# Pooled-key attention with a mixture of adapters: queries of chunks 4 to 7 turned by DMA, scores moved into the start, and the second batch's preparation re-timed

## The chip, the cores and the metric

The kernel runs on one core of a Trainium2 chip. The engines of the core run side by side, each through its own instruction list in order: TensorE (PE in the profile; its weight loads are PEld), VectorE (DVE), ScalarE (ACT), GpSimd (POOL), and SyncE (SP), which here issues nearly all DMAs. The metric is the device time of one execution in microseconds, taken as the median of several executions. The profile is one execution with every instruction recorded.

## The reference

There are four batches of 12288 queries with 128 columns. The keys and values of a batch are its kv image, averaged over 4x4 blocks to 768 rows and multiplied by `w_sr`. Softmax attention is followed by eight rank-16 adapters, of which each token uses its two best:

```python
kv_pool = kv.reshape(B, H // r, r, W // r, r, C).mean(axis=(2, 4))
kv_flat = kv_pool.reshape(B, -1, C) @ w_sr
a = softmax(scale * (q @ kv_flat.transpose(0, 2, 1)))
x = a @ kv_flat
logits = x @ w_gate             # the two largest of 8, softmax over them: w
out = x + sum over the two experts e of w[e] * (x @ A[e]) @ B[e]
```

## The kernel before

**Tiling.** The 49152 queries are cut into 96 chunks of 512, 24 per batch. A batch's keys are three tiles of 256 rows. One unit of score work, `scores(c, r)` (L295), multiplies chunk c's turned queries `qT` with key tile r on PE (two matmuls into a bank pair `sg`; there are two such pairs) and ACT takes the exponentials out of it into `tt` (L304). `weigh(c, h)` (L306) multiplies half of the exponentials with the values `vext` into `xps`, 12 matmuls each. `normalise(c)` (L319) is DVE work: a reciprocal (L322), the scaled copy `xn` (L326), and four searches for the largest logits, `top` (L333). Since `xps` exists once, the next chunk's first `weigh` waits for `xn`.

**The main loop** (L653) runs over c = 2 to 94; one pass is called period c here. It takes three units of score work from a list in order (`next_scores`), weighs chunk c-1, normalises it, turns the chunk before it for the adapters (`turned`, L373), and, with a lag of nine periods at first, multiplies by the adapters' first factor (`gated_hidden`) and second (`up`). The chunk's adapter weights go as follows. In every even period POOL runs `gate` for two chunks (five short instructions, L342 to L346), which needs DVE's `top` of that period. In the odd period after it, behind the second unit of score work, ACT runs a tanh over the result (`gate_tanhs`, L358). DVE then turns it (L402), and it goes out and comes back through DRAM.

**Queries.** A half of 1024 queries (two chunks) is loaded as fp32 by SP (`load_q`), cast to fp16 by POOL (`cast_q`, L107, in even periods behind `gate`), and turned by a DMA transpose on SP's queue (`turn_q`, L114). There are two fp32 buffers `q32`, so a load waits on SP's queue for the cast of two halves before. The first eight chunks do not go this way: they come in two loads `q0` and `q1`, and PE turns them (`queries`, L567), with ACT (chunks 0 to 3) or DVE (4 to 7) copying them to `qT`.

**Keys and values.** Each tile of a batch's kv image is loaded in four rows of 512 KB. Three additions join the rows (`sum_row`, L173) and two join the columns (`sum_cols`, L177, L178). DVE does this for batch 0, before the loop; POOL does it for the later ones. `plan(b)` (L255) fixes the periods: `at` for the loads, `sm` for the sums, `st` for the three steps on PE and ACT, which are the pooled transpose with its copy (`kp`, L189 and L191, at the period in `st`), values (L197, L199, two periods later) and keys (L205, L207, three periods later). In the loop `prep(c)` issues loads and sums, behind the gate and the cast of that period. `squares` (L236) is POOL work on values that a range check at the end needs.

**The start.** Tiles 0 to 2 of batch 0 become keys one after the other as their rows land (`tile_keys`, `tile_values`, written out from L603 on). Between them stand the query turns, the first scores and, as filler, plain matmuls (`warm`). Nine units of score work stand before the loop, and the loop takes one extra unit at the end of periods 6 and 8 (L717).

Of the kernel before, what the change touches and what calls it, by code (L numbers as in the profile page):

```python
# [10 lines left out]
FP32 = mybir.dt.float32  # L11
# [4 lines left out]
AF = mybir.ActivationFunctionType  # L16
# [5 lines left out]
def kernel(  # L22
# [10 lines left out]
    nc = tc.nc  # L33
    P = 128
    B, N, C = q.tensor.shape
# [5 lines left out]
    NTOK = 512  # L41
# [56 lines left out]


    def load_q(i):  # L100
        q32[i] = qpool.tile([P, 2, NS * C], FP32, tag="q32", name="q32", bufs=2)
        nc.sync.dma_start(q32[i], qflat[i * HROWS:(i + 1) * HROWS].rearrange(
            "(k p s) c -> p k (s c)", p=P, s=NS))

    def cast_q(i):
        q16[i] = qpool.tile([P, HROWS], F16, tag="q16", name="q16", bufs=3)
        nc.gpsimd.tensor_copy(q16[i], q32[i].rearrange("p k n -> p (k n)"))  # L107

    def new_qT(i):
        qT[i] = qpool.tile([P, 2 * NS, P], F16, tag="qT", name="qT", bufs=5)  # L110
# [1 line left out]
    def turn_q(i):  # L112
        new_qT(i)
        nc.sync.dma_start(qT[i], q16[i], transpose=True)  # L114
# [3 lines left out]
    for t in range(NT):  # L118
        load_kv(0, t)
        if t == 0:  # L120

            nc.sync.dma_start(q0, qflat[0:GROWS].rearrange("(k p s) c -> p k s c", p=P, s=NS))
    nc.sync.dma_start(q1, qflat[GROWS:2 * GROWS].rearrange("(k p s) c -> p k s c", p=P, s=NS))

    w_in = const.tile([P, P], FP32)
    nc.scalar.dma_start(w_in, w_sr)
# [53 lines left out]
    def stile(name):  # L180
        return ps_s.tile([P, 2, NTOK], FP32, tag="sg", name=name)
# [27 lines left out]
    def tile_keys(t, between=lambda: None):  # L209

        k = slice(2 * t * P, 2 * (t + 1) * P)
        kp_ps = ps_t.tile([P, 2 * P], FP32, tag="tp", name="kp_ps")
        for u in range(2):
            mm(kp_ps[:, u * P:(u + 1) * P], kvt[0, t][:, 0, u, 0:C], id_f32, is_transpose=True,
               start=(u == 0), stop=(u == 1), skip_group_check=True)
        if t < NT - 1:
            nc.scalar.activation(kpT[0][:, k], kp_ps, AF.Copy)
        else:
            nc.vector.tensor_copy(kpT[0][:, k], kp_ps)
        between()  # L220
        k_ps = mtile([P, 2 * P], name="k_ps")
        mm(k_ps, w_sr_sb, kpT[0][:, k], start=True, stop=True)
        nc.scalar.activation(kfT[0][:, k], k_ps, AF.Copy)

    def tile_values(t):
        v_ps = mtile([P, 2, C + E], name="v_ps")
# [28 lines left out]
    def plan(b):  # L255
        c0 = CPB * (b - 1)
        if b == 1:
            at = [2, 2, 3, 4, 5, 6, 6, 8, 9, 10, 10, 12]
            sm = [5, 5, 7, 9, 9, 11, 13, 13, 15]
            st = [10, 14, 18]  # L260
        else:
            at = [-11, -9, -7, -5, -5, -3, -1, 1, 1, 3, 5, 7]
            sm = [-3, -1, 1, 3, 5, 7, 9, 11, 13]
            st = [4, 10, 16]
        for i, k in enumerate(at):
            loads.setdefault(c0 + k, []).append((b, i // 4, i % 4))
# [28 lines left out]
    def scores(c, r):  # L295
        b = c // CPB
        if r == 0:
            tt[c] = ttpool.tile([P, NJ, NTOK], F16, tag="tt", name="tt")
        qc = qT[c // 2][:, c % 2 * NS:(c % 2 + 1) * NS].rearrange("p s t -> p (s t)")
        sg = stile("sg")  # L300
        for k in range(2):
            j = 2 * r + k
            mm(sg[:, k], kfT[b][:, j * P:(j + 1) * P], qc, start=True, stop=True)  # L303
        nc.scalar.activation(tt[c][:, 2 * r:2 * r + 2], sg, AF.Exp, bias=0.0, scale=scale)  # L304
# [253 lines left out]

    for i in range(4):
        new_qT(i)

    def queries(g, k, t):

        for i in range(NS):
            mm(t[:, i * P:(i + 1) * P], (q0, q1)[g][:, k, i], id_f32, is_transpose=True,  # L567
               start=(i == 0), stop=(i == NS - 1), skip_group_check=True)
        qt = qT[2 * g + k // 2][:, k % 2 * NS:(k % 2 + 1) * NS].rearrange("p s t -> p (s t)")
        if g == 0:  # L570
            nc.scalar.activation(qt, t, AF.Copy)
        else:
            nc.vector.tensor_copy(qt, t)
# [13 lines left out]
    a_bf = const.tile([P, P], BF16)  # L587
    b_half = const.tile([P, P], FP32)
    b_bf = const.tile([P, P], BF16)
    load_q(4)  # L590
    load_q(5)
    cast_q(4)
    for t in range(NT):
        for d in range(1, 4):
            sum_row(0, t, d, nc.vector)
        sum_cols(0, t, nc.vector)
        if t == 0:
            nc.vector.tensor_copy(a_bf.rearrange("p (r e) -> p e r", e=E),
                                  a_f.rearrange("p (e r) -> p e r", e=E))
# [3 lines left out]
    tile_keys(0, lambda: queries(0, 0, x_bank()))  # L603
    queries(0, 1, x_bank())
    scores(0, 0)
    tile_values(0)
    queries(0, 2, x_bank())
    scores(1, 0)
    queries(0, 3, x_bank())
    scores(2, 0)  # L610
    scores(3, 0)
    warm(8)
    tile_keys(1)
    warm(2)
    scores(0, 1)
    tile_values(1)
    scores(1, 1)
    weigh(0, 0)
    warm(2)
    tile_keys(2, lambda: queries(1, 0, stile("q_ps")[:, 0]))  # L620
    queries(1, 1, t_bank())
    scores(0, 2)
    tile_values(2)
    scores(2, 1)
    queries(1, 2, t_bank())
    weigh(0, 1)
    scores(1, 2)
    normalise(0)

    todo = [(x, r) for x in range(2, NCH) for r in range(3) if (x, r) not in ((2, 0), (2, 1), (3, 0))]

    def next_scores():
        if todo:
            scores(*todo.pop(0))

    NQ = NCH // GRP

# [12 lines left out]
    for c in range(2, NCH - 1):  # L653
        b, k = divmod(c, CPB)
        if c in fetched and lag(2 * fetched[c] + 1) > 8:
            load_gates(fetched[c])
        if c % 2 == 0 and c // 2 + 3 < 2 * NQ:
            turn_q(c // 2 + 3)
        if c % 2 and (c + 11) // 2 < 2 * NQ:
            load_q((c + 11) // 2)  # L660
        if c == 2:
            load_q(6)
        next_scores()
        if c == 2:
            queries(1, 3, t_bank())
        weigh(c - 1, 0)
        if c == NCH - 2:
            down(c - 4, stile("h_ps")[:, 0])
            apply_gate(c - 4)
        next_scores()  # L670
        if c >= 3 and c % 2 == 1:
            gate_tanhs((c - 3) // 2)
        for x in made.get(c, ())[:-1]:
            gated_hidden(x, t_bank())
        for x in ups.get(c, ()):
            up(x, None if x == ups[c][-1] else t_bank())
# [12 lines left out]
        _, evacuate = turned("x", c - 2)  # L689
        if c == NCH - 2:  # L690
            _, evacuate_h = turned("h", c - 4, stile("t_ps")[:, 0])
        next_scores()
        prep(c)
        if k in (17, 19, 21) and b + 1 < B:
            if b == 0:
                squares(0, (k - 17) // 2)
            squares(b + 1, (k - 17) // 2)
        if c in (32, 40, 56, 80):
            ranges((32, 40, 56, 80).index(c))
        a = slice(0, CUT * NS)  # L700
        if CUT < c <= CUT + 3:
            count_ok(a, c - CUT - 1, flags[:, 0:1])
        elif c == CUT + 4:
            values_ok()
        elif c == CUT + 5:
            count_sum(1)
        for x in made.get(c, ())[-1:]:
            gated_hidden(x)
        if c in sent:
            send_gates(sent[c])  # L710
        if c == NCH - 2:
            down(c - 3, stile("h_ps")[:, 0])
            apply_gate(c - 3)
        evacuate(c == NCH - 2)
        if c == NCH - 2:
            evacuate_h(True)
        if c in (6, 8):  # L717
            next_scores()

# [285 lines left out]
```

## Time and profile before

| | |
|---|---|
| median of 3 runs | 381.48 us (381.07 to 382.75) |
| the profiled execution | 382.61 us, its span 380.8 us |
| PE busy | 362.9 us (95%) |
| ACT, DVE, POOL busy | 311.1, 301.7, 224.4 us |
| DMA moved | 100.47 MB, mean 264 GB/s |

In rows of the timeline the first number is the start in us from the span's start and the second the length; in square brackets stands how long the engine had been idle before and what ended that. Rows of one kind that follow each other are merged, with their count at xN. PE's matmuls overlap in the pipeline, so a row is longer than the time by which it delays the next one. SPq is SP's queue issuing a DMA. In the view by windows each row has the stretch, its length, the busy time of each engine in it, the granted PE clock, the DMA share and GB/s.

### The profile page before, as it was taken

The numbers are of one execution on the slowest core, as the hardware profiler recorded it, in microseconds if no ns is written. First come the engines' busy times: TensorE is split into PE (matmuls) and PEld (weight loads), VectorE is DVE, ScalarE is ACT, GpSimd is POOL, SyncE is SP. The second block draws the span as 40 slices with busy tenths as digits, with TensorE's granted clock in tenths as the row PEclk, the third lists the DMA queues.
The fourth block names the chain that finished last, engine by engine and source line by source line (L and its number), as shares of the span: only waits on it lengthen the run. The fifth ranks groups of instructions, "written<-read, shape, count | busy, mean of one in ns | idle before, by whom it ended". The sixth has DMA issues, their size and how long they took to land.

```text
span 380.8 us, 10632 instructions
## 1 busy us (share of the span) xinstructions
PE 362.9 (95%) x3962; PEld 267.7 (70%) x3963; DVE 301.7 (79%) x951; ACT 311.1 (82%) x392; POOL 224.4 (59%) x374
## 2 busy tenths in 40 slices
PE   4989989999999999999999999999999999999993
PEld 1447757677777777777777777777777777767682
DVE  2686556878788888888888888888888898898983
ACT  1547999888888888888888988988888888888853
POOL 1002699996898877764689877755524335232244
PEclk9999999999999999999999999999999999999998
DMA  8996799999999999999999999999899799883325
GB/s 253 364 386 205 203 271 303 300 310 256 365 296 302 309 326 259 312 288 320 320 289 304 338 279 299 278 246 243 175 298 256 196 226 243 182 220 119 136 86 195
DMA packets 93465, 100.47 MB, mean 264 GB/s; under 512 B 56676, under 2 KB 56932, under 8 KB 93412
## 3 DMA queue, kind: packets, MB, share of 16 engines
q1 hardware_dynamic: 91940, 99.58, 96.1%
q8 instruction: 31, 0.51, 0.6%
q10 hardware_dynamic: 1472, 0.20, 0.3%
q14 instruction: 22, 0.18, 0.1%
HBM read 62.33 MB, written 25.90 MB: 232 GB/s over the span
## 4 chain that ended last, share of the span: by engine, by line
PE 73%; DMA 9%; DVE 7%; POOL 7%; issue 2%; ACT 1%; SPq 0%; ACTq 0%; POOLq 0%; DVEq 0%
PE xps L315 30%; PE sg L303 26%; PE d_ps L463 5%; PE t_ps L382 4%; DMA kvt<-in_kv_dram 4%; PE h_ps L417 4%; DMA b_f<-in_moe_B_dram 3%; POOL kvt L173 2%; DVE xn L326 2%; DMA ge<-g_h 2%; DVE ht L420 1%; PE v_ps L197 1%; DVE top L333 1%; POOL q L107 1%; POOL kvt L177 1%
## 5 line engine op out<-in xcount | busy, mean ns | idle before, releaser
L304 ACT ACTIVATE tt<-sg 128x1024 f16<-128x1024 f32 x288 | 277.5, 1022 | 34.8 <-PE sg L303 33.9
L303 PE MATMUL sg<-qT,kfT 128*128 128x512 f16 x576 | 170.1, 379 | 2.4 <-ACT tt L304 1.6
L315 PEld LDWEIGHTS <-tt 128*128 128x128 f16 x2304 | 148.0, 98 | 27.0 <-DVE xn L326 17.2
L315 PE MATMUL xps<-vext,tt 128*128 128x137 f16 x2256 | 166.3, 223 | 0.0
L477 DVE TENSOR_TENSOR osb<-d_ps,xn 128x512 f32<-128x512 f32 x85 | 58.7, 691 | 30.6 <-PE d_ps L463 30.4
L342 POOL TENSOR_TENSOR arg<-xn,top 128x64 f32<-128x64 f32 x47 | 14.8, 315 | 107.3 <-DVE top L333 91.5
L326 DVE TENSOR_TENSOR xn<-xps,rinv_all 128x548 f32<-128x548 f32 x94 | 68.5, 728 | 3.2
L303 PEld LDWEIGHTS <-kfT 128*128 128x128 f16 x576 | 49.3, 98 | 27.1 <-issue 3.9
L173 POOL TENSOR_TENSOR kvt<-kvt 128x1024 f32<-128x1024 f32 x27 | 63.8, 2362 | 0.2
L107 POOL CAST q<-q 128x1024 f16<-128x1024 f32 x44 | 45.7, 1038 | 26.6 <-DMA q<-in_q_dram 26.6
L420 DVE SCALAR_TENSOR_TENSOR ht<-ge,h_ps 128x512 bf16<-128x512 f16 x87 | 58.5, 672 | 0.6 <-DMA ge<-g_h 0.3
L463 PEld LDWEIGHTS <-ht 128*128 128x128 bf16 x368 | 27.2, 97 | 23.6 <-DVE ht L420 3.9
L333 DVE MAX8 top<-xn 128x8 f32<-128x8 f32 x376 | 35.1, 156 | 6.3
L393 DVE COPY xt<-t_ps 128x512 bf16<-128x512 bf16 x92 | 36.7, 399 | 0.0
L382 PE MATMUL t_ps<-id_bf,xn 128*128 128x128 bf16 x376 | 36.3, 219 | 0.0
L463 PE MATMUL d_ps<-b_bf,ht 128*128 128x128 bf16 x340 | 32.9, 219 | 0.3 <-DVE ht L420 0.2
L417 PE MATMUL h_ps<-xt,a_bf 128*128 128x512 bf16 x86 | 32.6, 379 | 0.1
L322 DVE RECIPROCAL rinv_all<-xps 128x4 f32<-128x4 f32 x94 | 17.1, 182 | 15.4 <-PE xps L315 13.1
L382 PEld LDWEIGHTS <-xn 128*128 128x128 bf16 x376 | 26.0, 98 | 0.3
L345 POOL TENSOR_SCALAR msk<-msk 128x64 f32<-128x64 f32 x47 | 20.2, 429 | 4.1
L346 POOL TENSOR_TENSOR arg<-arg,msk 128x64 f32<-128x64 f32 x47 | 15.1, 321 | 3.9
L344 POOL TENSOR_TENSOR arg<-arg,msk 128x64 f32<-128x64 f32 x47 | 15.0, 320 | 3.7
(149 smaller groups left out, 229.4 us busy)
## 6 DMA issues: line engine op xcount, KB each, us to landing
kvt<-in_kv_dram SPq DMA_DIRECT2D x48, 512.0 KB
q<-in_q_dram SPq DMA_DIRECT2D x44, 512.0 KB
out_dram<-osb SPq DMA_DIRECT2D x44, 512.0 KB
ge<-g_h SPq DMA_DIRECT2D x45, 256.0 KB
q<-in_q_dram SPq DMA_DIRECT2D x2, 1024.0 KB
out_dram<-osb SPq DMA_DIRECT2D x8, 256.0 KB
g_h<-g_sb SPq DMA_DIRECT2D x45, 16.0 KB
qT<-q SPq DMA_TRANSPOSE x44
```

Source lines behind the costliest of these rows:

```text
L107: nc.gpsimd.tensor_copy(q16[i], q32[i].rearrange("p k n -> p (k n)"))
L173: eng.tensor_tensor(v[:, 0], v[:, 0], v[:, d], op=ALU.add)
L303: mm(sg[:, k], kfT[b][:, j * P:(j + 1) * P], qc, start=True, stop=True)
L304: nc.scalar.activation(tt[c][:, 2 * r:2 * r + 2], sg, AF.Exp, bias=0.0, scale=scale)
L315: mm(o, tt[c][:, j, s * P:(s + 1) * P], vext[b][:, j, 0:VW], start=(j == 0 and s % 2 == 0), stop=(j == NJ - 1 and s % 2 == 1), skip_group_ ...
L326: nc.vector.tensor_tensor(xn[c].rearrange("p (b s) v -> p b s v", b=2), xv, ri.rearrange("p (b s) -> p b s", b=2).unsqueeze(3).broadcast_t ...
L333: nc.vector.max(gin[c // 2][:, (c % 2) * NS + s], xn[c][:, s, C:C + E])
L382: mm(columns(t_ps, c, s), src[:, s], id_bf, is_transpose=True, start=(s == 0), stop=(s == NS - 1), skip_group_check=True)
L417: mm(h_ps, a_bf, xT[c], start=True, stop=True)
L420: nc.vector.scalar_tensor_tensor(hgT[c].rearrange("p (k a) t -> p k (a t)", k=2), gE[c // 2][:, h:h + NS // 2].rearrange("p a t k -> p k ( ...
L463: mm(dps[c][:, s], columns(hgT[c], c, s), b_bf, start=(s == 0 and fresh), stop=(s == NS - 1), skip_group_check=True)
L477: nc.vector.tensor_tensor(osb[:, lo:hi], d, xn[c][:, lo:hi, 0:C], op=ALU.add)
```

## The change

Five things change together.

- Chunks 4 to 7 no longer go through PE. Their load is split into halves 2 and 3 (`load_half`), issued in the order half 2, half 4, half 3, half 5. DVE casts half 2 in two pieces (`cast_half`), POOL casts half 3 ahead of half 4, and SP issues two more DMA transposes ahead of the one for half 4. `q32` gets three buffers. All 16 query transposes of chunks 4 to 7 on PE and their four DVE copies are gone.
- `scores(2, 1)` and `scores(3, 1)` stand between the steps that make tile 2's keys; `kfT` of tile 2 is copied by DVE instead of ACT; one more unit, (2, 2), stands ahead of the loop. So 11 units stand before the loop, and the extra units of periods 6 and 8 are gone. Four of the filler matmuls are gone too.
- The second batch's sums move from periods 5, 5, 7, 9, 9, 11, 13, 13, 15 to 3, 5, 6, 8, 9, 10, 12, 14, 16, and their loads with them.
- Its steps start at periods 9, 13 and 19 instead of 10, 14 and 18.
- The squares of batches 0 and 1 move from periods 17, 19, 21 to 19, 21, 23.

```diff
     def load_q(i):
-        q32[i] = qpool.tile([P, 2, NS * C], FP32, tag="q32", name="q32", bufs=2)
+        q32[i] = qpool.tile([P, 2, NS * C], FP32, tag="q32", name="q32", bufs=3)
...
-    nc.sync.dma_start(q1, qflat[GROWS:2 * GROWS].rearrange("(k p s) c -> p k s c", p=P, s=NS))
+    def load_half(i):
+        q32[i] = q1[:, 2 * i - 4:2 * i - 2].rearrange("p k s c -> p k (s c)")
+        nc.sync.dma_start(q32[i], qflat[i * HROWS:(i + 1) * HROWS].rearrange(
+            "(k p s) c -> p k (s c)", p=P, s=NS))
+
+    load_half(2)
+    load_q(4)
+    load_half(3)
+    load_q(5)
...
-        nc.scalar.activation(kfT[0][:, k], k_ps, AF.Copy)
+        if t < NT - 1:
+            nc.scalar.activation(kfT[0][:, k], k_ps, AF.Copy)
+        else:
+            nc.vector.tensor_copy(kfT[0][:, k], k_ps)
...
-            at = [2, 2, 3, 4, 5, 6, 6, 8, 9, 10, 10, 12]
-            sm = [5, 5, 7, 9, 9, 11, 13, 13, 15]
-            st = [10, 14, 18]
+            at = [2, 2, 3, 4, 5, 5, 6, 8, 9, 9, 11, 13]
+            sm = [3, 5, 6, 8, 9, 10, 12, 14, 16]
+            st = [9, 13, 19]
...
-    load_q(4)
-    load_q(5)
+    new_q16(2)
+    cast_q(3)
     cast_q(4)
+
+    def cast_half(k):
+        nc.vector.tensor_copy(q16[2][:, k * NTOK:(k + 1) * NTOK], q32[2][:, k])
...
-    warm(8)
+    warm(6)
     tile_keys(1)
...
-    warm(2)
-    tile_keys(2, lambda: queries(1, 0, stile("q_ps")[:, 0]))
-    queries(1, 1, t_bank())
+    def during():
+        cast_half(0)
+        scores(2, 1)
+
+    tile_keys(2, during)
+    cast_half(1)
+    turn_q(2)
+    turn_q(3)
+    scores(3, 1)
     scores(0, 2)
     tile_values(2)
-    scores(2, 1)
-    queries(1, 2, t_bank())
+    scores(1, 2)
     weigh(0, 1)
-    scores(1, 2)
+    next_scores()
     normalise(0)
...
-        if c == 2:
-            queries(1, 3, t_bank())
...
-        if k in (17, 19, 21) and b + 1 < B:
+        k0 = 19 if b == 0 else 17
+        if k in (k0, k0 + 2, k0 + 4) and b + 1 < B:
             if b == 0:
-                squares(0, (k - 17) // 2)
-            squares(b + 1, (k - 17) // 2)
+                squares(0, (k - k0) // 2)
+            squares(b + 1, (k - k0) // 2)
...
-        if c in (6, 8):
-            next_scores()
```

More of the change, by code (lines that the diff above doesn't have):

```diff
@@ L105, in cast_q, with new_q16 @@
     def cast_q(i):
+        new_q16(i)
+        nc.gpsimd.tensor_copy(q16[i], q32[i].rearrange("p k n -> p (k n)"))
+    def new_q16(i):
         q16[i] = qpool.tile([P, HROWS], F16, tag="q16", name="q16", bufs=3)
-        nc.gpsimd.tensor_copy(q16[i], q32[i].rearrange("p k n -> p (k n)"))
     def new_qT(i):
@@ L557, in all_ok, with queries @@
         nc.vector.tensor_scalar(bad, last, tot, full, op0=ALU.add, op1=ALU.not_equal)
-    for i in range(4):
+    for i in range(2):
         new_qT(i)
-    def queries(g, k, t):
+    def queries(k, t):
         for i in range(NS):
-            mm(t[:, i * P:(i + 1) * P], (q0, q1)[g][:, k, i], id_f32, is_transpose=True,
+            mm(t[:, i * P:(i + 1) * P], q0[:, k, i], id_f32, is_transpose=True,
                start=(i == 0), stop=(i == NS - 1), skip_group_check=True)
[L569 to L573, printed above, removed]
+        qt = qT[k // 2][:, k % 2 * NS:(k % 2 + 1) * NS].rearrange("p s t -> p (s t)")
+        nc.scalar.activation(qt, t, AF.Copy)
     def x_bank():
@@ L602, with next_scores @@
     warm(18)
-    tile_keys(0, lambda: queries(0, 0, x_bank()))
-    queries(0, 1, x_bank())
+    todo = [(x, r) for x in range(2, NCH) for r in range(3) if (x, r) not in ((2, 0), (2, 1), (3, 0), (3, 1))]
+    def next_scores():
+        if todo:
+            scores(*todo.pop(0))
+    tile_keys(0, lambda: queries(0, x_bank()))
+    queries(1, x_bank())
     scores(0, 0)
     tile_values(0)
-    queries(0, 2, x_bank())
+    queries(2, x_bank())
     scores(1, 0)
-    queries(0, 3, x_bank())
+    queries(3, x_bank())
     scores(2, 0)
     scores(3, 0)
-    warm(8)
+    warm(6)
     tile_keys(1)
@@ L618 @@
     weigh(0, 0)
-    warm(2)
-    tile_keys(2, lambda: queries(1, 0, stile("q_ps")[:, 0]))
-    queries(1, 1, t_bank())
+    def during():
[6 more added lines that the diff above has]
+    scores(3, 1)
     scores(0, 2)
     tile_values(2)
-    scores(2, 1)
-    queries(1, 2, t_bank())
+    scores(1, 2)
     weigh(0, 1)
-    scores(1, 2)
+    next_scores()
     normalise(0)
[L633 to L637, printed above, removed]
     NQ = NCH // GRP
```

## The prediction

> **What bounds the kernel now.** I write R(k) for the start of the reciprocal of chunk k, which marks the periods. First the page's totals, then the view by windows with each window running from one reciprocal to the next, then the timeline around what that shows.
>
> ```profile
> span 380.8 us, 10632 instructions
> PE 362.9 (95%) x3962; PEld 267.7 (70%) x3963; DVE 301.7 (79%) x951; ACT 311.1 (82%) x392; POOL 224.4 (59%) x374
> ```
> ```profile
> 44.51:47.59 3.08, 3.08 (x38) 2.16 (x36) 1.70 (x8) 3.06 (x5) 3.08 (x3) 1.00 0.89 240
> 47.59:51.83 4.24, 3.58 (x40) 2.44 (x38) 1.61 (x8) 4.01 (x5) 4.00 (x6) 1.00 1.31 311
> 51.83:55.01 3.18, 3.18 (x38) 2.19 (x36) 1.70 (x8) 2.93 (x5) 3.10 (x4) 1.00 0.86 129
> 55.01:59.30 4.29, 3.57 (x40) 2.44 (x38) 1.61 (x7) 3.94 (x5) 3.92 (x7) 1.00 1.04 377
> 66.32:70.14 3.82, 3.55 (x41) 2.60 (x39) 2.99 (x10) 2.99 (x5) 3.65 (x5) 1.00 1.16 258
> 74.06:77.97 3.91, 3.72 (x43) 2.71 (x41) 2.99 (x10) 3.44 (x6) 3.75 (x5) 1.00 1.18 269
> 88.99:92.89 3.90, 3.72 (x43) 2.71 (x41) 2.99 (x10) 3.44 (x6) 2.61 (x5) 1.00 1.51 173
> 110.78:114.28 3.50, 3.50 (x43) 2.60 (x41) 2.99 (x10) 2.99 (x5) 3.42 (x4) 1.00 1.11 337
> 149.31:152.93 3.62, 3.62 (x45) 2.78 (x44) 2.90 (x9) 3.27 (x5) 1.87 (x6) 1.00 1.21 221
> 152.93:156.33 3.40, 3.40 (x41) 2.57 (x39) 2.99 (x10) 3.09 (x5) 3.08 (x2) 1.00 1.15 342
> 156.33:160.24 3.91, 3.91 (x47) 3.07 (x47) 3.00 (x9) 3.28 (x5) 2.16 (x6) 1.00 1.11 303
> 160.24:163.81 3.57, 3.57 (x45) 2.73 (x43) 2.99 (x11) 3.37 (x6) 3.49 (x3) 1.00 1.23 215
> ```
>
> Undisturbed periods are PE's: 3.40 us, 3.62 with a `kp` step, 3.91 with values, 3.57 with keys (last four rows). Before the adapter work begins (period 9) a period is 3.08, and there ACT is full too (3.06 of 3.08). The two rows of 4.24 and 4.29 hold the extra score units: ACT is the longer engine in them and PE idles 0.7. They cost 1.16 and 1.21 over 3.08. The rows 51.83 (0.10 over 3.08), 66.32 (0.42 over 3.40), 74.06 and 88.99 (0.34 and 0.33 over 3.57) and 110.78 (0.10) are stalls too: together 1.29. Their cause is POOL:
>
> ```profile
> 41.43 0.18 DVE L322 RECIPROCAL rinv_all<-xps 128x4 f32<-128x4 f32 x1 [1.31 <-PE xps L315]
> ...
> 42.86 0.31 POOL L342 TENSOR_TENSOR arg<-xn,top 128x64 f32<-128x64 f32 x1 [3.27 <-DVE top L333]
> ```
> ```profile
> 65.36 0.31 POOL L342 TENSOR_TENSOR arg<-xn,top 128x64 f32<-128x64 f32 x1
> ```
> ```profile
> 66.32 0.18 DVE L322 RECIPROCAL rinv_all<-xps 128x4 f32<-128x4 f32 x1
> ...
> 67.29 0.32 ACT L358 ACTIVATE gw_all<-arg 128x64 f16<-128x64 f32 x1 [0.83 <-DVE xn L326]
> ```
>
> A gate on time starts 1.43 after its reciprocal (41.43 to 42.86). The one at 65.36 is late, POOL having been at sums, and ACT sits 0.83 idle at the tanh, which it had reached 0.14 after the reciprocal at 66.32. PE loses 0.42 of these 0.83, so about 0.4 is absorbed by the two `sg` banks and ACT's slack. A gate on time therefore has 0.2 to spare: it is ready 1.43 + 1.9 = 3.33 after its reciprocal, and wanted at 3.40 + 0.14 = 3.54.
>
> ```profile
> 101.34 0.31 POOL L342 TENSOR_TENSOR arg<-xn,top 128x64 f32<-128x64 f32 x1 [1.07 <-DVE top L333]
> ...
> 103.19 1.04 POOL L107 CAST q<-q 128x1024 f16<-128x1024 f32 x1
> 104.19 2.36 POOL L173 TENSOR_TENSOR kvt<-kvt 128x1024 f32<-128x1024 f32 x1
> 106.50 0.64 POOL L241 TENSOR_TENSOR sq<-vext 128x272 f32<-128x272 f16 x1
> ...
> 109.50 0.31 POOL L342 TENSOR_TENSOR arg<-xn,top 128x64 f32<-128x64 f32 x1
> ```
> ```profile
> 83.14 2.36 POOL L173 TENSOR_TENSOR kvt<-kvt 128x1024 f32<-128x1024 f32 x1
> ...
> 87.60 0.31 POOL L342 TENSOR_TENSOR arg<-xn,top 128x64 f32<-128x64 f32 x1
> ```
>
> POOL's price list, start to start: gate 1.85, cast 1.0, a sum 2.31, four squares 3.0, a sum with both column additions 4.46. A pair of periods (even, odd) holds one gate and one cast, 2.85.
>
> **The change part by part.**
>
> *Extra units gone.* Both periods return to 3.08: -2.37. The units have to fit into the start instead.
>
> ```profile
> 27.74 0.42 DVE L219 COPY kp_keep<-kp_ps 128x256 f32<-128x256 f32 x1 [0.53 <-PE kp_ps L214]
> ...
> 28.22 0.70 PE L222 MATMUL k_ps<-kp_keep,w_sr_sb 128*128 128x256 f32 x2
> ...
> 28.95 0.38 ACT L223 ACTIVATE kfT<-k_ps 128x256 f16<-128x256 f32 x1 [1.47 <-PE k_ps L222]
> 28.97 1.04 POOL L107 CAST q<-q 128x1024 f16<-128x1024 f32 x1 [26.65 <-DMA q<-in_q_dram]
> ...
> 30.04 1.94 ACT L304 ACTIVATE tt<-sg 128x1024 f16<-128x1024 f32 x2 [0.70 <-PE sg L303]
> 30.04 1.36 SPq L114 DMA_TRANSPOSE qT<-q  x1
> ...
> 31.17 0.88 PE L315 MATMUL xps<-vext,tt 128*128 128x137 f16 x12
> ...
> 33.19 0.88 PE L315 MATMUL xps<-vext,tt 128*128 128x137 f16 x12
> ```
>
> *The start.* Tile 2's `kp` is bound by DVE's sums and stays. (2, 1) runs on PE in the wait for the 0.42 copy, its exponential (0.97 of two in 1.94) on ACT from 28.3; (3, 1) runs behind `k_ps`, its exponential to 30.3. DVE's `kfT` ends as ACT's did, near 29.4, if the first `cast_half` fits between 28.16 and 28.95. The exponential of (0, 2) then starts at 30.3 instead of 30.04, and chunk 0's second `weigh` (31.17) is 0.25 late. The next `weigh` (33.19) waits for `xn`, not for PE; so the turns taken off PE behind 29 buy nothing there, and +0.25 stays. Price of each turn if it were on the path: about 0.44. The four fillers lay in idle time; without them PE's longest added wait is 0.4.
>
> *DMA.* SP issues two transposes (1.36 each) ahead of the one it issued at 30.04. Half 3 lands in the place where half 4 landed, so POOL casts it from 28.97, then half 4 to 31.0. The first transpose starts at about 29.9, behind the second `cast_half`. (128x512 from SBUF on DVE has no row. The nearest, 128x256 from PSUM, is 0.42; I take 0.43, between 0.3 and 0.7.)
>
> On POOL: two casts where it was idle for 26.65 ahead of its first: nothing.
>
> ```profile
> GB/s 346 49 5 0 171 157 202 340 405 364 328 302 36 0 0 59 161 374 420 342 147 76 331 358 287 328 346 349 328 171 49 26 105 394 410 410 376 381 330 202
> ```
> ```profile
> SPq L102 <- POOL q L107: 20.1, 10, 6.2
> ```
>
> This is the DMA view from 28 to 60 us in slices of 0.8. The transpose issued at 30.04 is the 171, 157 from 31.2; the 4.8 us behind it are 1.5 MB (one query half, two key rows); then the queue is empty until 40, because SP waits for a cast to free one of two buffers (6.2 is the longest such wait). Three buffers end that wait, so the two added transposes mostly fill this hole. Chunk 4's queries land at about 33 and are wanted at 34.1. The two rows of the first sum land at 31.1 + 3 x 1.6 + 4.8 = 40.7, if each transpose takes 1.6 as this one.
>
> *First sum in period 3.* POOL is free for it at 39.8, so it waits for the rows: 40.7 + 2.31 = 43.0, just when the next gate is due (41.66 + 1.43 = 43.1, R(3) being 0.25 late). Later rows cost one for one, for in the 3.08 stage nothing absorbs them. Bounds: transposes of 1.6 (nothing) to 3.2 us, as the one at 50.4 to 53.6 in that row (rows at 45.5, 4.8 lost). I take 0.35, under half a slice, since the two transposes that have only loads ahead of them show 1.6.
>
> *Spread sums.* The pair (4, 5) is 2.85 + 2.31, under 6.16. The pair (6, 7) is 2.85 + 4.46 = 7.31: the gate of period 8 is 1.15 late. The tanh of period 9 then ends at R(8) + 1.7, and now a `kp` copy stands behind it:
>
> ```profile
> 62.50 0.39 PE L189 MATMUL kp_ps<-id_f,kvt 128*128 128x128 f32 x2
> ...
> 62.92 0.39 ACT L191 ACTIVATE kp_keep<-kp_ps 128x256 f32<-128x256 f32 x1
> ...
> 63.59 0.59 PE L303 MATMUL sg<-qT,kfT 128*128 128x512 f16 x2
> ```
>
> The copy (0.39) holds a score bank that PE wants 1.09 after the step, at R(8) + 0.9; it comes at R(8) + 2.05: +1.15. The pair (8, 9) is 2.85 + 4.62 against 3.08 + 4.77: the gate of period 10 is 0.8 late, its tanh stands ahead of the copy of the values: +0.25. The pair (10, 11), 7.31 of 7.56, and the later ones fit. With 0.35 from above: +1.75. The five old stalls go: -1.29. Steps on PE cost the same in their new periods, and their sums are done 0.4 or more ahead.
>
> *Squares.* They now meet sums in two pairs running. (20, 21): 2.85 + 2.31 + 3.0 = 8.16 against 3.40 + 3.91 = 7.31, late 0.85; ACT waits 0.5, PE 0.1. (22, 23): 8.16 against 3.57 + 3.50, late 1.95; ready at 1.43 + 1.95 + 1.9 = 5.3, wanted at 3.54; of 1.75 PE loses 1.3. (24, 25): 7.31 against 6.8 + 1.3, late 1.15, loses 0.5. Sum +1.9. Bounds: 0, if ACT's waits are absorbed, to 3.1, if nothing is.
>
> The Trainium skill, "SBUF — State Buffer", section "Who interferes with whom", says that VectorE in a two-port mode and GpSimd exclude each other from a shared pair of SBUF ports for a whole instruction. The second `cast_half` would then wait for POOL's cast to end at 30.01, half 2's transpose and the rows would come 0.6 later, and the sum below would be 0.6 more, 382.3. No row here shows two such copies at once, so this is an estimate.
>
> **Sum.** -2.37 + 0.25 + 1.75 - 1.29 + 1.9 = +0.24 on the profiled execution of 382.61, so 382.85. This execution lies 1.13 above the median of the runs, 381.48; on that scale 381.7.
>
> **The rivals.**
>
> *Late gates are absorbed (faster).* If ACT's queue hides late gates in the new places, 1.4 and 1.9 vanish and 378.4 remains; with the squares alone hidden, 379.8. For it: the gate at 109.50 was 0.7 late and cost 0.10. Against: the one at 65.36, late 1.3, cost 0.42.
>
> *Transposes hold the first sum (slower).* If three transposes in a row take 3.2 each, the rows land at 45.5, POOL waits, the gate behind is 4.8 late, and ACT and PE stop at once: 386.1. It decides, past 0.5%, once the rows land after 42.7. For it: the slow one at 50.4. Against: that one was preceded by more than loads.
>
> *The two units do not get in.* If chunk 4's queries land after 34.1, PE stands at (4, 0) and the units gained are waited for again: landing at 34.7 (one slow transpose) gives 382.3.
>
> **How the numbers follow.** My forecast 0.55, with a range of its own of 379.8 to 383.3; absorbed 0.20; first sum held 0.20; units not in 0.05. About 0.5% (1.9 us) is what a measurement of this kernel can tell from no change. The forecast and the last rival lie within it. Of the forecast's share I put 0.06 beyond it on the slow side and 0.02 on the fast one, since the terms for the first sum and the squares have such bounds. That gives faster 0.22, same 0.52, slower 0.26. The range 378.6 to 384.4 leaves out the lower part of the absorbed case and the upper half of the held one.
>
> **What would show it.** Periods 6 and 8 at 3.08; R(1) at about 35.5; period 9 near 4.8; ACT idle about 1.7 at the tanh of period 25 and POOL without a gap from R(20) on to period 26; ahead of the squares the chunks about 1.7 earlier than before, behind them level. Rows landing past 42.7, or no idle ACT at period 25, would prove me wrong.

## The result and the profile after

The changed kernel takes 382.83 us (median of 20 runs, 381.90 to 384.57), the kernel before 381.25 us (20 runs, 380.90 to 382.75). The ratio is 1.0036, 95% interval 1.0023 to 1.0049: slower by 1.4 us (1.6 by the medians), and within the 0.5% that I had called no change. I had said 381.7, or 0.2 over the kernel before.

The profiled execution of the changed kernel took 382.04 us, its span 380.3: less than the profiled one of before, though the kernel is slower. So the traces are compared piece by piece. First the page's totals after:

```profile
span 380.3 us, 10586 instructions
PE 360.6 (95%) x3943; PEld 265.1 (70%) x3943; DVE 300.3 (79%) x950; ACT 310.5 (82%) x391; POOL 225.5 (59%) x375
```

Then the view by windows, before and after, each in three pieces: first reciprocal to second, second to that of chunk 47, and on to that of chunk 93.

```profile
32.09:35.26 3.17, 3.17 (x38) 2.60 (x37) 1.92 (x7) 2.66 (x3) 0.00 (x0) 1.00 0.88 279
35.26:198.68 163.42, 161.35 (x1814) 121.06 (x1813) 127.79 (x427) 145.84 (x182) 128.85 (x185) 1.00 1.11 295
198.68:362.67 163.99, 163.18 (x1845) 121.21 (x1843) 141.80 (x456) 140.72 (x172) 83.68 (x154) 1.00 0.92 237
```
```profile
30.31:33.40 3.09, 2.91 (x34) 2.05 (x33) 1.29 (x7) 2.77 (x4) 0.00 (x0) 1.00 1.22 175
33.40:198.28 164.88, 161.08 (x1811) 120.56 (x1809) 127.84 (x428) 143.76 (x180) 128.81 (x185) 1.00 1.08 302
198.28:361.99 163.71, 162.99 (x1845) 121.30 (x1843) 141.66 (x455) 140.79 (x172) 83.69 (x154) 1.00 0.85 233
```

PE has 0.27 us less to do in the middle piece (161.35 to 161.08) and takes 1.46 longer for it. From the first reciprocal to that of chunk 93, the changed kernel is 1.10 slower (-0.08, +1.46, -0.28). The first reciprocal came 1.78 earlier (30.31 against 32.09), and most of this is no gain of the start. DVE's copy of tile 2's `kp` is itself 1.76 earlier. Of what was changed, only the four filler matmuls and the split of the query load stood ahead of it:

```profile
25.98 0.42 DVE L231 COPY kp_keep<-kp_ps 128x256 f32<-128x256 f32 x1 [0.53 <-PE kp_ps L226]
26.32 0.42 DVE L607 CAST q<-q 128x512 f16<-128x512 f32 x1
27.19 0.42 DVE L238 CAST kfT<-k_ps 128x256 f16<-128x256 f32 x1 [0.46 <-PE k_ps L234]
27.54 0.85 DVE L607 CAST q<-q 128x512 f16<-128x512 f32 x1
```

From this copy to the first reciprocal it is 4.33 now and was 4.35 (27.74 to 32.09). In the profiled run of before a key row had landed late, with DVE waiting for it in the timeline, and that run was 1.4 us above its median:

```profile
19.65 1.23 DVE L173 TENSOR_TENSOR kvt<-kvt 128x1024 f32<-128x1024 f32 x1 [1.44 <-DMA kvt<-in_kv_dram]
```

There is one more profiled execution with the old start, that of the new plan alone (below). In it no row was late in this place, and the copy began at 26.76:

```profile
26.76 0.42 DVE L219 COPY kp_keep<-kp_ps 128x256 f32<-128x256 f32 x1 [0.85 <-PE kp_ps L214]
```

In the eleven executions with the new start it began between 25.86 and 26.42. DVE waited 0.85 ahead of it here, not 0.53, because PE was still at two of the fillers (25.91 to 26.34) when the sums were done. So up to 0.3 of the 1.76 may be a gain of the start after all, by the fillers; one execution doesn't settle it.

Where the 1.46 lies is seen period by period (same view; period c runs from the reciprocal of chunk c-1 to that of chunk c; the periods 6, 8, 9, 11, 5, 19, 23, 25, 27 and 13 in this order):

```profile
47.02:50.10 3.08, 3.08 (x38) 2.16 (x36) 1.60 (x7) 2.85 (x4) 2.04 (x6) 1.00 1.01 376
53.19:56.27 3.08, 3.08 (x36) 2.16 (x34) 1.60 (x7) 2.85 (x4) 2.92 (x5) 1.00 1.35 254
56.27:61.05 4.78, 3.94 (x45) 2.81 (x44) 2.99 (x10) 3.72 (x6) 4.45 (x7) 1.00 0.97 339
64.45:68.66 4.21, 4.07 (x47) 3.06 (x47) 3.05 (x10) 3.45 (x6) 4.03 (x4) 1.00 1.01 345
42.66:47.02 4.36, 3.25 (x38) 2.20 (x36) 1.80 (x9) 3.05 (x5) 4.11 (x7) 1.00 0.91 304
93.78:97.54 3.76, 3.76 (x45) 2.78 (x44) 2.99 (x11) 3.46 (x6) 2.51 (x4) 1.00 0.84 283
108.41:111.98 3.57, 3.56 (x43) 2.61 (x41) 3.00 (x11) 2.99 (x5) 3.49 (x4) 1.00 0.83 278
115.37:120.15 4.78, 3.56 (x43) 2.60 (x41) 3.08 (x11) 3.00 (x5) 4.53 (x8) 1.00 0.96 318
123.55:127.46 3.91, 3.55 (x41) 2.59 (x39) 2.98 (x10) 2.98 (x5) 3.74 (x5) 1.00 1.08 375
72.22:76.11 3.89, 3.78 (x45) 2.78 (x44) 2.99 (x10) 3.44 (x6) 3.73 (x4) 1.00 1.09 373
```

Gained: 1.16 and 1.21 in periods 6 and 8. Lost: 1.28 in period 5 (over 3.08), 1.16 in period 9 (over 3.62, the `kp` step being there now), 0.30 in period 11 (over 3.91), 0.27 in period 13 (over 3.62), 0.14 in period 19 (over 3.62), and behind the squares 0.17, 1.38 and 0.51 in periods 23, 25 and 27 (over 3.40), 2.06 together. With the five stalls of before gone (1.29), this adds up to 1.55, against the 1.46 of the piece.

In the timeline, POOL around the loss in period 5, and ACT at the tanhs of periods 5, 9, 11, 25 and 27:

```profile
36.69 1.04 POOL L107 CAST q<-q 128x1024 f16<-128x1024 f32 x1
40.15 2.36 POOL L185 TENSOR_TENSOR kvt<-kvt 128x1024 f32<-128x1024 f32 x1 [2.42 <-PE t_ps L397]
42.46 0.31 POOL L357 TENSOR_TENSOR arg<-xn,top 128x64 f32<-128x64 f32 x1
```
```profile
44.39 0.32 ACT L373 ACTIVATE gw_all<-arg 128x64 f16<-128x64 f32 x1 [1.31 <-POOL arg L361]
...
57.69 0.32 ACT L373 ACTIVATE gw_all<-arg 128x64 f16<-128x64 f32 x1 [0.99 <-POOL arg L361]
57.91 0.36 ACT L203 ACTIVATE kp_keep<-kp_ps 128x256 f32<-128x256 f32 x1
...
65.29 0.32 ACT L373 ACTIVATE gw_all<-arg 128x64 f16<-128x64 f32 x1 [0.70 <-POOL arg L361]
...
117.30 0.32 ACT L373 ACTIVATE gw_all<-arg 128x64 f16<-128x64 f32 x1 [1.78 <-POOL arg L361]
...
124.61 0.32 ACT L373 ACTIVATE gw_all<-arg 128x64 f16<-128x64 f32 x1 [0.93 <-POOL arg L361]
```

POOL was free at 37.7 and sat idle for 2.42 until the first sum could begin. So the gate at 42.46 is 1.46 later than 1.43 after its reciprocal (39.57). At the five tanhs ACT waits 1.31, 0.99, 0.70, 1.78 and 0.93 for POOL.

### The profile page after: what moved, and what is told of

Its sections match the earlier page's. It is cut to its first block, busy times and chain, and to the rows that moved or that the text cites. A ratio compares the mean times of both kernels' runs of the same rounds, so it can differ in the third digit from the quotient of the medians.

```text
span 380.3 us, 10586 instructions
## 1 busy us (share of the span) xinstructions
PE 360.6 (95%) x3943; PEld 265.1 (70%) x3943; DVE 300.3 (79%) x950; ACT 310.5 (82%) x391; POOL 225.5 (59%) x375
## 4 chain that ended last, share of the span: by engine, by line
PE 68%; POOL 13%; DVE 8%; DMA 5%; issue 3%; ACT 2%; ACTq 0%; SPq 0%; POOLq 0%; DVEq 0%
PE xps L330 28%; PE sg L318 24%; PE d_ps L478 5%; PE t_ps L397 4%; PE h_ps L432 4%; POOL kvt L185 4%; DMA kvt<-in_kv_dram 3%; DMA b_f<-in_moe_B_dram 3%; DVE xn L341 2%; POOL q L107 1%; DVE ht L435 1%; POOL msk L360 1%; POOL kvt L189 1%; ACT tt L319 1%; DVE kvt L185 1%
## 5 line engine op out<-in xcount | busy, mean ns | idle before, releaser
L107 POOL CAST q<-q 128x1024 f16<-128x1024 f32 x45 | 46.8, 1042 | 24.9 <-DMA q<-in_q_dram 24.7
L373 ACT ACTIVATE gw_all<-arg 128x64 f16<-128x64 f32 x45 | 14.1, 314 | 7.4 <-POOL arg L361 7.3
L361 POOL TENSOR_TENSOR arg<-arg,msk 128x64 f32<-128x64 f32 x47 | 15.1, 321 | 3.9
```

## The experiments

All ratios are to the kernel before, run on the same chip. Differences to the changed kernel are of medians, some of them from another chip, where the kernel before took 381.41 to 381.49. A "period" in these expectations is counted by its reciprocal, as in the prediction.

### The key rows ahead of query half 6

```diff
-        if c == 2:
-            load_q(6)
         next_scores()
         weigh(c - 1, 0)
...
         prep(c)
+        if c == 2:
+            load_q(6)
```

> The changed kernel, but in period 2 the two key rows are put ahead of the load of query half 6 on SP's queue. Theory: the first sum of period 3 waits on POOL for its second row (the sum began 2.42 after POOL was free, and the gate behind it came 1.46 late), so rows that land 1.3 to 1.5 earlier let the gate start 1.43 after its reciprocal, the period that was 4.36 becomes 3.08 to 3.15, and the kernel loses about 1.2 against the changed one: 0.3 over the kernel before. Rival: the sum waits for what the trace names, the turn of a chunk on PE (t_ps), or the time comes from the transposes and not from POOL: then the sum begins where it did, 0.6 after its reciprocal, the period stays at 4.36 and the kernel 1.4 over the kernel before.

Measured: 381.26 us, ratio 0.9993 (0.9985 to 1.0002), 1.6 below the changed kernel. POOL and period 5 in it:

```profile
38.61 2.36 POOL L185 TENSOR_TENSOR kvt<-kvt 128x1024 f32<-128x1024 f32 x1 [1.00 <-issue]
40.92 0.32 POOL L357 TENSOR_TENSOR arg<-xn,top 128x64 f32<-128x64 f32 x1
```
```profile
42.53:45.62 3.09, 3.09 (x38) 2.17 (x36) 1.70 (x8) 3.08 (x5) 3.09 (x3) 1.00 0.89 283
```

The sum began 1.54 earlier, the gate 1.47 behind its reciprocal, and period 5 fell from 4.36 to 3.09. The rows were the cause, and the releaser that the trace named (PE's turn) was not. All that was saved stayed saved.

### The squares apart

```diff
-        k0 = 19 if b == 0 else 17
-        if k in (k0, k0 + 2, k0 + 4) and b + 1 < B:
-            if b == 0:
-                squares(0, (k - k0) // 2)
-            squares(b + 1, (k - k0) // 2)
+        for s in {19: ((0, 0), (0, 1), (0, 2)), 21: ((1, 0),), 23: ((1, 1),), 39: ((1, 2),)}.get(c, ()):
+            squares(*s)
+        if b > 0 and k in (17, 19, 21) and b + 1 < B:
+            squares(b + 1, (k - 17) // 2)
```

> The changed kernel, but the squares of batch 0 all in period 19, those of batch 1 in 21, 23 and 39, where POOL has room. Theory: the squares behind the sums made the gates late and cost 0.13 (period 19), 0.17 (23), 1.37 (25) and 0.52 (27), 2.2 in all; without them these periods are 3.62, 3.40, 3.40 and 3.40 and the kernel is 2.2 below the changed one, 0.8 below the kernel before. Rival: the loss there comes from the second batch's sums and the third batch's being brought close together, not from the squares: then period 25 stays over 4.4 and less than 0.7 is gained.

Measured: 380.23 us, ratio 0.9969 (0.9958 to 0.9980), 2.6 below the changed kernel. Periods 23, 25 and 27 in it:

```profile
108.41:111.80 3.39, 3.39 (x43) 2.56 (x41) 2.98 (x10) 3.08 (x5) 3.39 (x3) 1.00 0.83 232
115.20:118.60 3.40, 3.40 (x43) 2.57 (x41) 2.99 (x11) 3.09 (x5) 3.32 (x3) 1.00 1.15 229
122.00:125.39 3.39, 3.39 (x41) 2.56 (x39) 2.98 (x10) 3.00 (x5) 3.31 (x4) 1.00 1.17 306
```

All three are undisturbed. The theory holds for them, the rival falls. Period 19 stayed at 3.75, so the 0.13 that the theory counted there is not the squares'. In the changed kernel the gate of period 18 begins at 92.24, 1.85 behind its reciprocal and so 0.42 late, behind the sum and the column additions planned for period 16, and the tanh of period 19, with a `kp` copy behind it, waits 0.25 for it. In the run with the steps a period later (below) this gate comes 1.50 behind its reciprocal, the squares are the same, and period 19 is 3.61.

### The new start alone

The loads, sums, steps and squares are those of the kernel before:

```diff
-            at = [2, 2, 3, 4, 5, 5, 6, 8, 9, 9, 11, 13]
-            sm = [3, 5, 6, 8, 9, 10, 12, 14, 16]
-            st = [9, 13, 19]
+            at = [2, 2, 3, 4, 5, 6, 6, 8, 9, 10, 10, 12]
+            sm = [5, 5, 7, 9, 9, 11, 13, 13, 15]
+            st = [10, 14, 18]
...
-        k0 = 19 if b == 0 else 17
-        if k in (k0, k0 + 2, k0 + 4) and b + 1 < B:
+        if k in (17, 19, 21) and b + 1 < B:
...
-            squares(b + 1, (k - k0) // 2)
+            squares(b + 1, (k - 17) // 2)
```

> The new start and query transposes alone: sums, loads, steps and squares at the periods of the kernel before. Theory: the extra units gone are worth 2.4 and the start nothing more (0.1), the five stalls of the old plan (1.3) stay: 2.4 to 2.5 below the kernel before, ratio 0.9935. Rival: the old stalls grow, since the chunks reach period 5 earlier but the key rows, behind two more transposes, do not: the two sums of period 5 then hold the gate of period 6 by more, and 0.5 to 1.5 of the 2.4 is lost.

Measured: 381.18 us, ratio 0.9992 (0.9984 to 1.0001). Of the 2.4 at most 0.6 is left by this interval, and nothing is clear of noise; the rival is right that the old stalls grow, and by more than it said, but not in its reason: the two sums of period 5 begin at 44.08, right behind the cast, and wait for no rows. Periods 7 and 9 are now 4.33 and 4.46 (3.18 and 3.40 before). The reason is seen in POOL's stretches without a gap. In the timeline of POOL alone, these are two rows ahead of which it waited, with no such row between them, for the kernel before and then for this one:

```profile
42.86 0.31 POOL L342 TENSOR_TENSOR arg<-xn,top 128x64 f32<-128x64 f32 x1 [3.27 <-DVE top L333]
94.39 0.31 POOL L342 TENSOR_TENSOR arg<-xn,top 128x64 f32<-128x64 f32 x1 [2.71 <-DVE top L333]
```
```profile
41.23 0.31 POOL L357 TENSOR_TENSOR arg<-xn,top 128x64 f32<-128x64 f32 x1 [3.27 <-DVE top L348]
92.75 0.31 POOL L357 TENSOR_TENSOR arg<-xn,top 128x64 f32<-128x64 f32 x1 [2.71 <-DVE top L348]
```

Before, POOL works without a gap from 42.86 to 94.39 - 2.71 = 91.68; with the new start from 41.23 to 90.04. Both are 48.8 us. From period 4 to period 17 POOL was the bound of the kernel before, at a mean of 59% busy over the span. The time of the long periods 6 and 8 was POOL's as well, and so taking it from PE and ACT gives nothing by itself.

### The new plan alone

The kernel before with the changed kernel's `at`, `sm`, `st` and squares.

> The kernel before with the second batch's new sums, loads and steps and the squares two periods later; the old start, chunks 4 to 7 on PE, and the extra units of periods 6 and 8 stay. Theory: the long periods 6 and 8 (1.2 more than 3.08 each) are time that POOL also has, so that the gate of period 8 is not late there, and the first sum's rows, with no transposes ahead, land in time: only the squares (2.2) and some 0.3 at period 11 come, the old stalls (1.3) go: about 1.0 to 1.3 over the kernel before, ratio 1.003. Rival: the two parts of the change simply add: the changed kernel less the one with the new start alone is 1.65, and so this one is 1.6 over the kernel before or more, with period 9 over 4.6 in it.

Measured: 382.51 us, ratio 1.0026 (1.0016 to 1.0036), 1.0 over the kernel before. Period 9 is 3.79, with the `kp` step in it, not 4.78; period 5 is 3.09; periods 23, 25 and 27 lose 0.15, 1.37 and 0.51 as in the changed kernel. So in the old start the plan costs little but the squares: the time of the long periods 6 and 8 was POOL's too. The theory holds in the main (the 0.3 at period 11 didn't come; it is 3.92). By the ratios the parts don't quite add (start alone -0.0008, plan alone +0.0026, both +0.0036), but the gap of 0.0018 is no wider than the three intervals together allow; that the parts depend on each other is shown by period 9 (3.79 and 4.78) and period 5 (3.09 and 4.36).

### The column additions on DVE

```diff
-            if d == 3:
+            if d == 3 and (b, t) != (1, 0):
                 sum_cols(b, t, nc.gpsimd)
+        if c == 8:
+            sum_cols(1, 0, nc.vector)
```

> The changed kernel, but the two column additions of the first new tile (2.15 on POOL) are done by DVE in period 8. Theory: they make the gate of period 8 1.15 late, and its tanh holds the kp copy in period 9: without them this period is 3.62 instead of 4.78 and the kernel 1.16 below the changed one, 0.2 over the kernel before. Rival: the kp step itself, put into period 9 while ACT is nearly full, costs it: then the period stays over 4.4.

Measured: 381.98 us, ratio 1.0021 (1.0006 to 1.0037). Period 9 fell to 4.20, half of what I expected; it is neither 3.62 nor over 4.4. A part of the other half is seen in POOL's gate, which ran beside DVE's column additions (54.09 to 55.2):

```profile
54.31 0.62 POOL L359 TENSOR_TENSOR arg<-xn,top 128x64 f32<-128x64 f32 x1 [1.04 <-DVE top L350]
54.88 0.50 POOL L360 TENSOR_TENSOR msk<-xn,top 128x64 f32<-128x64 f32 x1
```

The gate began on time, but two of its instructions took 0.62 and 0.50 where they take 0.31. The Trainium skill, "SBUF — State Buffer", section "Who interferes with whom", says that a VectorE instruction with two SBUF inputs contends with a GpSimd instruction that reads SBUF. The trace agrees, with 0.5 us for this gate.

ACT waited 0.42 at the tanh, and PE, waiting for the `kp` copy behind it, lost about 0.35 of the 0.58 by which the period is over 3.62. The other 0.24 is the rival's: the first score matmul behind the `kp` step starts 0.45 after the turn ahead of it (55.92 to 56.37), where 0.22 is usual. It starts as ACT's third exponential ends (56.32), ahead of the tanh. The changed kernel has the same 0.24 there (56.29 to 56.75). So both theories have a share.

### The steps a period later

```diff
-            st = [9, 13, 19]
+            st = [10, 14, 19]
```

> The changed kernel, but the first two tiles' steps (kp, values, keys) start in periods 10 and 14 instead of 9 and 13, so that no copy stands behind the tanh of periods 9 and 11; the sums stay, and with them the late gates. Theory: a late gate alone costs what ACT waits less about 0.4, and only the kp copy behind the tanh, which holds a score bank, makes it cost in full: period 9 falls from 4.78 to 3.9 to 4.1, period 11 loses 0.2 to 0.3 beyond its values (0.51), the kp step itself (0.22) goes to period 10, and the kernel is 0.6 to 0.9 below the changed one. Rival: ACT's wait at the tanh costs in full wherever it is, since ACT and PE are both nearly full: then period 9 stays at 4.5 or more, and under 0.3 is gained.

Measured: 383.01 us, ratio 1.0033 (1.0017 to 1.0048): no gain, against 0.6 to 0.9. Period 9 is 4.25 without a `kp` copy in it. So the late gate alone cost 0.85 there, ACT having waited 0.97, and the `kp` step with its copy some 0.3. My price, wait less 0.4, would have been 0.57. The 0.3 was given back: period 11, which held values in the changed kernel and holds none now, is 3.95, and period 13 is 4.06 against 3.89. The changed kernel and this one, each from a gate that POOL had waited for to the end of the stretch that follows, by windows:

```profile
48.45:76.00 27.55, 26.46 (x297) 19.57 (x295) 18.28 (x64) 24.19 (x32) 26.06 (x33) 1.00 1.13 310
```
```profile
49.54:77.10 27.56, 26.08 (x294) 19.45 (x293) 18.37 (x64) 23.87 (x31) 26.06 (x33) 1.00 1.10 296
```

27.55 and 27.56, with 33 POOL instructions and 26.06 busy in both. POOL is the bound of this stretch as well. A price by single waits tells at most in which period the lateness reaches PE. Over the stretch POOL's work sets the time, and the edit had not changed it.

In this run's profile period 5 took 5.31, the first sum having begun at 41.25, 1.53 behind its reciprocal (0.58 in the changed kernel's). It was 4.36, 4.40 and 3.99 in other runs with the same loads. The 0.95 by which the rows came later than in the changed kernel is passed on in full (5.31 against 4.36).

### Both pieces of half 2 cast before POOL begins

```diff
     def during():
         cast_half(0)
+        cast_half(1)
         scores(2, 1)
...
     tile_keys(2, during)
-    cast_half(1)
```

> The changed kernel, but DVE casts both pieces of half 2 one after the other, ahead of the copy of tile 2's keys, before POOL's cast of half 3 begins. Theory: the second piece took 0.85 instead of 0.42 because POOL's cast ran beside it; alone it takes 0.42, the first transpose is issued up to 1.1 earlier (27.3 to 27.6 instead of 28.41), the rows of the first sum land as much earlier, and period 5, 4.36 in the changed kernel, falls to 3.3 to 3.6: the kernel 0.8 to 1.0 below the changed one. Rival: 0.85 belongs to the second piece itself (its place in memory, or what lands there at the same time): it stays 0.85. Second rival: the rows land when they did, since the loads ahead of them set the time: period 5 stays over 4.1.

Measured: 382.13 us, ratio 1.0021 (0.9994 to 1.0047), 0.7 below the changed kernel by the medians, but with overlapping intervals. DVE's two casts, SP's queue and POOL in it:

```profile
26.45 0.75 DVE L607 CAST q<-q 128x512 f16<-128x512 f32 x2
```
```profile
27.23 5.03 SPq L117 DMA_TRANSPOSE qT<-q  x3
32.31 0.58 SPq L102 DMA_DIRECT2D q<-in_q_dram  x1
32.99 1.22 SPq L87 DMA_DIRECT2D kvt<-in_kv_dram  x2
```
```profile
40.39 2.35 POOL L185 TENSOR_TENSOR kvt<-kvt 128x1024 f32<-128x1024 f32 x1 [2.53 <-PE sg L318]
```

The first rival falls: each piece took 0.42, the two overlapping to 0.75, and the first transpose was issued at 27.23 instead of 28.41. The second rival is right in what it forecast: the sum began at 40.39, no earlier, and period 5 was 4.48. So the 0.7, if it is real, doesn't come from period 5. The three issues took 5.03 on SP instead of 4.13, so the loads behind them were issued only 0.3 to 0.6 earlier, and landed no earlier. The first issue took 2.31 of the 5.03, against 1.37 in the changed kernel. What made it slower the runs don't settle; the DMA was still busy with loads until about 28.

### Both edits, and a plan by POOL's time

First the two edits that won (rows first, squares apart) in one kernel:

> The changed kernel with both edits that won, the key rows ahead of query half 6 and the squares apart. Theory: the two terms lie 15 periods apart and add: 1.57 and 2.6 below the changed one, so about 378.7, ratio 0.993 to the kernel before. Rival: what is gained early is waited for again later (PE is ahead of the adapter weights that come back through DRAM), and the ratio stays at 0.996 or above.

Measured: 379.27 us, ratio 0.9943 (0.9930 to 0.9956), 3.6 below the changed kernel. The rival falls. The two add to within 0.6 (1.6 and 2.6 alone); 0.4 of this is seen in the profiled run, in period 29 (3.81 against 3.40), where PE waited for a transposed query half.

Then the sums by what POOL has free:

```diff
-            at = [2, 2, 3, 4, 5, 5, 6, 8, 9, 9, 11, 13]
-            sm = [3, 5, 6, 8, 9, 10, 12, 14, 16]
-            st = [9, 13, 19]
+            at = [2, 2, 3, 5, 5, 6, 8, 9, 11, 11, 12, 13]
+            sm = [3, 5, 7, 8, 10, 12, 14, 15, 16]
+            st = [10, 14, 19]
...
+        if c == 8:
+            sum_cols(1, 0, nc.gpsimd)
         for b, t, d in sums.get(c, ()):
             sum_row(b, t, d, nc.gpsimd)
-            if d == 3:
+            if d == 3 and (b, t) != (1, 0):
                 sum_cols(b, t, nc.gpsimd)
...
+        for s in {19: ((0, 0), (0, 1)), 21: ((0, 2),), 23: ((1, 0),), 27: ((1, 1),), 39: ((1, 2),)}.get(c, ()):
```

> The kernel with both edits, and the second batch planned by POOL's free time: sums in periods 3, 5, 7, 8, 10, 12, 14, 15, 16, the first tile's column additions apart from its last sum (period 8), steps from 10, 14 and 19, the squares in 19, 21, 23, 27 and 39. Theory: no pair of periods then has over 0.9 more on POOL than its time and no copy stands behind a late tanh: period 9 falls from 4.78 to 3.40 (the kp step, 0.22, moves to 10), period 11 loses up to 0.3, and the kernel is 1.0 to 1.5 below the one with both edits, ratio 0.989 to 0.991. Rival: the later sums, now closer together, make late gates of their own in periods 11, 15 and 17 and take back more than half.

Measured: 379.40 us, ratio 0.9960 (0.9937 to 0.9983), no better than the two edits alone. Period 9 fell to 3.40 and 11 to 3.40 as expected. But period 14 became 5.29, for a reason that neither theory had:

```profile
74.15 0.72 POOL L190 TENSOR_TENSOR kvt<-kvt 128x256 f32<-128x256 f32 x1
```
```profile
74.93 0.44 PE L201 MATMUL kp_ps<-id_f,kvt 128*128 128x128 f32 x2 [1.46 <-POOL kvt L190]
```

PE stood 1.46 for the second tile's column additions: I had moved its last sum by two periods (10 to 12) and its steps by one (13 to 14). So the steps a period later, at 15:

> The kernel with both edits and the plan by POOL's free time, with the second tile's steps at 15 instead of 14, since its column additions ended 1.46 after PE wanted them. Theory: period 14 falls from 5.29 to 3.40, periods 15 and 18 hold the steps, nothing else moves: 377.5 to 377.9, ratio 0.990. Rival: POOL's stretch without a gap, from 67.5 to 82.6 there, sets the time, and the loss moves to the next gate: no more than 0.6 is gained.

Measured: 378.36 us, ratio 0.9916 (0.9883 to 0.9948), 1.0 below the run before by the medians, between the theory and its rival. Period 14 is 3.40, and period 17 loses 0.10 (4.01 over 3.91). The same with the first tile's steps at 11:

> As the run before, but the first tile's steps from 11 instead of 10. Theory: in period 10 PE waited some 0.24 for the column additions; a period later it does not, but the kp copy then stands behind the tanh of a gate that is 0.8 late, which costs 0.3 to 0.8 in period 11: equal to the run before or up to 0.5 slower. Rival: the late gate is absorbed there as it was without the copy (period 11 was 3.40): 0.2 faster.

Measured: 378.10 us, ratio 0.9930 (0.9903 to 0.9957), equal within the intervals. Period 10 lost its 0.24, and period 11 became 4.11, 0.49 over a `kp` period, as expected of a copy behind a late tanh. Both are faster than the kernel before, by 0.7 to 0.8%, and than the changed one.

## Why the prediction was right, and where it wasn't

No change clear of 0.5% was forecast, and none came: 0.2 over the kernel before forecast, 1.4 measured, within the range. The sum itself was short by 1.2. That the answer stood is owed in part to the width of the 0.5% (1.9 us) and to misses of both signs. By its steps:

- **Extra units gone** (-2.37): periods 6 and 8 are 3.08 each, as forecast. But that price holds only beside a plan that lets POOL keep up. Alone it is worth nothing clear of noise (ratio 0.9992), since POOL's 48.8 us without a gap covered it. I had read the five old stalls as separate waits, 1.29 in all. They were the edge of one bound, and the sentence "Both periods return to 3.08: -2.37" gave a gain to the start that belonged to both parts together.
- **The start** (+0.25): wrong, -0.10. The exponential of (0, 2) is late as reckoned, but the first reciprocal stands at the same distance, 4.33 against 4.35, and the second is 0.08 nearer. The step that failed is "the turns taken off PE behind 29 buy nothing there": before, the second `weigh` (31.17) stood behind such a turn (30.73), and counted from the `kp` copy it is 0.28 earlier now (29.13). And "the four fillers lay in idle time" holds for the profiled execution of before, but not for the one of the new plan alone, where two of them held the `kp` copy up by 0.3.
- **First sum** (+0.35): the term that was mis-sized, 1.28. The DMA's rate was right: in the view of the DMA of the changed kernel (slices of 0.8 from 28 us) three transposes fill six slices from 29.6, 1.6 each, and the gap is filled.

```profile
GB/s 0 0 178 171 212 179 92 150 347 371 241 374 389 346 366 430 383 211 36 113 378 407 399 422 410 410 352 277 198 361 399 399 373 273 119 44 343 353 371 407
```

  On SP's queue the three issues stand in one row:

```profile
28.41 4.13 SPq L117 DMA_TRANSPOSE qT<-q  x3
```

  What was late: by the `kp` copy, the sum was due 40.7 - 27.74 = 13.0 behind it and began 14.2 behind it. Of the 1.2, 0.3 is the first transpose, issued 2.43 behind the copy and not 2.16, the second cast having taken 0.85; the rest is left, by exclusion, for the loads behind the transposes. And chunk 3 was 0.35 earlier than reckoned, the start not having cost anything. The two add to the 1.5 by which the gate was late. "Later rows cost one for one" was right, as the runs with 3.99 to 5.31 for this period show.
- **Spread sums**: period 9 at 4.78 (4.77 forecast), period 11 +0.30 (+0.25). The sizes are right, and so are the places; the mechanism only in part. The `kp` step and its copy have 0.3 of the first; the rest is POOL's stretch without a gap. And "the later ones fit" was wrong: period 13 lost 0.27, since the gates were still late from the pairs before (the one at 70.82 by 0.73), and period 19 lost 0.14 behind the last sum.
- **Squares** (+1.9): 2.06 in periods 23, 25 and 27 (0.17, 1.38, 0.51; forecast 0.1, 1.3, 0.5), with ACT idle 1.78 at the tanh of period 25, where I said 1.7. PE lost wait less 0.4 there and in period 27 (0.51 of 0.93), as priced.
- **The profiled execution**: adding 0.24 to its 382.61 and then taking off 1.13 is the same as adding 0.24 to the median. That 382.85, the figure before the 1.13 was taken off, is so near the measured 382.83 is luck: the 1.13 belongs to that execution, in which a key row was late.

The sum was 0.24. What was missed by then (first sum 0.93, start -0.35, period 11 0.05, period 13 0.27, squares 0.16, period 19 0.14) makes it 1.44, and the 0.28 that the last piece of the trace lost, nearly all in period 85 (3.66 before, 3.40 now), makes it 1.16. The trace has 1.08 (1.10 less the 0.02 ahead of the first reciprocal), up to chunk 93.

Of the signs that the prediction named, periods 6, 8 and 9, ACT's wait of 1.78 and POOL without a gap (from 99.03 on, past period 26) came. R(1) was 33.40, or 35.16 with the 1.76 added. Counted from the `kp` copy, the chunks were 0.6 earlier than before ahead of the squares' cost (chunk 22), not 1.7, and 1.4 later behind it (chunk 28), not level.

Of the rivals, none came. Absorbed gates: the squares' cost came in full and went away with the squares. Slow transposes: they took 1.6 each. The first sum did wait for its rows, but began at 40.15, short of the 42.7 (40.9 by this run's earlier `kp` copy) from which that rival would have decided. It was near: in the profiled run with the steps a period later, which has the same start and the same loads, it began at 41.25. The late queries did not happen: PE had no wait for chunk 4.

The estimate by the rule of the Trainium skill, "SBUF — State Buffer", section "Who interferes with whom" (half 2's transpose 0.6 later), was borne out in part: the second cast began at 27.54 beside POOL's first (27.07 to 28.11), took 0.43 more than the first one and ended 0.28 behind POOL's; the transpose was issued 0.3 later than reckoned. POOL's next cast took 1.24 instead of 1.04.

## What to carry to other kernels

Look for stretches in which an engine has no gap, not only for its share of the span: POOL, at 59%, was the bound for 48.8 us, and there a gain of 2.4 us on PE and ACT was worth nothing clear of noise until POOL's work was moved. Price a plan by summing the engine's work between two points at which it waits, and carry lateness on until a gap takes it up. Before loads are put behind new DMA work, look at who waits for the last of them: here moving one load behind two key rows was worth 1.6 us.

## What I had not expected of the hardware

- A DVE cast of 128x512 from SBUF took 0.42 alone and 0.85 beside a POOL cast, and DVE's copy from PSUM 0.42 beside the same POOL cast (27.19). So it is not that DVE slows beside POOL as such.
- The price works the other way too: two POOL instructions of 0.31 took 0.62 and 0.50 beside DVE's column additions.
- Issuing three transposes on SP took 4.13 in one kernel and 5.03 in another that began 1.2 earlier, so that an earlier start of them bought nearly nothing; the cause is open.
